# Eight dK stores sent by GpSimd in three row pieces each, in place of five dV stores in two

## The chip, the cores and the metric

The kernel runs on one core of one Trainium2 chip. The metric is the device time of one execution in microseconds; the times of several executions are given by their median. Beside them stands one execution recorded by the hardware profiler, and every duration in this document that is not a median comes from such a recorded execution. A core has five engines that are named here: TensorE (PE, with its weight loads as PEld), VectorE (DVE), ScalarE (ACT), GpSimd (POOL) and SyncE (SP, which here only issues transfers). Sixteen DMA engines move the data between HBM and the on-chip memory.

## The reference

The reference is grouped-query attention and its gradients. For 32 batches there are 32 query heads with 4 query rows each, 4 key heads with 2048 keys, and head size 128; every key head serves 8 query heads.

```
scores = einsum("bhqd,bhkd->bhqk", q, k) * scale
p = softmax(scores)
out = einsum("bhqk,bhkd->bhqd", p, v)
dq, dk, dv = vjp(out, grad_out)
```

All inputs and outputs are bfloat16. K, V, dK and dV are the large ones: 64 MiB each; q, grad_out, out and dq are small.

## The kernel before

One batch is the unit of work, and 32 batches follow each other. The four key heads of a batch are taken in two pairs, g = 0 and 1. Outside the timed program K and V are laid out so that a pair of heads is one tile of 128 partitions x 4096 elements, which a load or a store moves as 128 rows of 8192 bytes. To each K tile 128 columns are appended that hold q (pair 0) or grad_out (pair 1), so that a K row has 8448 bytes (`LONG` = 4224 elements, against `ROW` = 4096). In the same way the output tile dv1 carries the attention output in its last 128 columns, and dk1 carries dq. A batch has four loads (k0, k1, v0, v1) and four stores (dk0, dk1, dv0, dv1), some 1 MiB each. They share 20 slots of 128 x 4224 elements on the chip (`slots`, named `row` in the profile): a slot holds a loaded tile, is later written with an output tile or another input, and can be loaded again only when its store has landed.

For every batch PE transposes K and V (L260, two bf16 values moved as one 32-bit word), computes the scores (L274), after which DVE (L279) and ACT (L283) make the exponentials, and PE computes the output (L312) and dV (L334). DP = grad_out times V (L274) gives dS on DVE (L327), and from dS come dQ (L312) and dK (L334). The results leave PSUM by copies on ACT and DVE (L340); dQ is scaled and copied by DVE into the last columns of the dk1 slot (L320, `row<-psum,rs`).

GpSimd does three small things in a batch: it scales grad_out by the softmax denominator (`dop`, L290), makes the factor for dQ (`rs`, L302) and scales q (`qp`, L293). PE needs `dop` for dV and `qp` for dK.

The order of the work is written out by hand in the string `PLAN`: four characters per unit (what, part, PSUM bank or slot or copying engine, tile), read from left to right under `manual_schedule`, so that every engine runs its instructions in exactly this order. Units of neighbouring batches are interleaved: around the dQ of batch b (`y`, `z`) stand the exponentials and the dV of batch b + 1, and `F1`, the store of dk1 of batch b, follows directly behind `z`, the copy of dQ.

Loads and stores are issued by SP (L245, L350, L346), in order; an instruction on SP that waits holds back all later ones. SP's transfers run in queue q1. Five stores are an exception: dv0 of the batches 4, 6, 8, 10 and 12 (`SPREAD`) is not issued by SP but by GpSimd as an indirect DMA (`scatter`, L201 to L203), in two pieces (`PIECES`): the last 2 rows, then the first 126. They stand behind `qp` of the next batch in GpSimd's order (L295 to L299) and run in queue q0. Two tiny scatters of 3 and 13 integers (`turns`) stand ahead of the first piece and behind the last one (L205, L299). The pieces go to outputs of their own, and are put into place outside the timed program.

```
def scatter(out, in_):
    nc.gpsimd.indirect_dma_start(out=out, in_=in_, in_offset=None,
                                 out_offset=bass.IndirectOffsetOnAxis(ap=at[0:in_.shape[0], 0:1], axis=0))
```

Of the kernel before, what the change touches and what calls it, by code (L numbers as in the profile page):

```python
# [16 lines left out]
ROW = 2 * 16 * P  # L17
LONG = ROW + P
# [1 line left out]
SLOTS, E_TILES, DS_TILES = 20, 2, 2  # L20
TILES = dict(KT=8, VT=7, ET=2, DT=2)

SPREAD = (4, 6, 8, 10, 12)
PIECES = ((126, 2), (0, 126))

NAMES = dict(
    a="LK", b="LV", c="QT", d="QTe", e="KT", f="KTe", g="VT", h="VTe", i="S", j="MX", k="EX", l="RC", m="dop", n="qp",
# [141 lines left out]
def kernel(  # L169
# [13 lines left out]
    nc = tc.nc  # L183
# [14 lines left out]
    at = const_pool.tile([P, 1], mybir.dt.int32, name="at")  # L198
    nc.gpsimd.iota(at[:], pattern=[[0, 1]], base=0, channel_multiplier=1)

    def scatter(out, in_):  # L201
        nc.gpsimd.indirect_dma_start(out=out, in_=in_, in_offset=None,
                                     out_offset=bass.IndirectOffsetOnAxis(ap=at[0:in_.shape[0], 0:1], axis=0))  # L203

    scatter(turns[0], at[0:3, 0:1])  # L205
    junk = const_pool.tile([P, D], BF16, name="junk")
    slots = [const_pool.tile([P, LONG], BF16, name=f"row{i}") for i in range(SLOTS)]
    tiles = {x: [const_pool.tile([P, 8 * P], BF16, name=f"{x.lower()}_sb{i}") for i in range(n)]
# [6 lines left out]
    T = collections.defaultdict(dict)  # L215
# [17 lines left out]
    def emit(u):  # L233
# [12 lines left out]
        elif name == "QT":  # L246
            ps = t["qtp"] = bank(u)[:, 0:P]
            for j, x in enumerate(("q", "go")):
                nc.tensor.transpose(out=ps.bitcast(BF16)[:, P * j:P * j + P], in_=t[x], identity=ident[:])  # L249
        elif name == "QTe":  # L250
            t["qdt"] = sm_pool.tile([P, 2 * P], BF16, name="qdt_sb", bufs=3)
            copy16(u.where, t["qdt"][:], t["qtp"])
        elif name in ("KT", "VT", "ET", "DT"):
            x, (half, h) = name[0], divmod(i, NH) if name in ("KT", "VT") else (i, None)
            t[name, i] = tiles[name][u.tile]
            ps = t[name + "p", i] = bank(u)
            src = t[x, h] if h is not None else t["e" if x == "E" else "ds"][:]
            src = src.bitcast(FP32).rearrange("p (j d) -> p j d", d=P)
            for j in range(4):
                nc.tensor.transpose(out=ps[:, P * j:P * j + P], in_=src[:, 4 * half + j, :], identity=ident32[:])  # L260
        elif name in ("KTe", "VTe", "ETe", "DTe"):
            copy16(u.where, t[name[:2], i][:], t[name[:2] + "p", i])
        elif name in ("S", "DP"):
            if name == "S" and i == 0:
                t["S"], t["e"] = bank(u, 4), e_sb[u.tile]
            if name == "DP":
                t["DP", i] = bank(u, 2)
                if i == 0:
                    t["ds"] = ds_sb[u.tile]
            out = t["S"][:, 2 * QW * i:2 * QW * i + 2 * QW] if name == "S" else t["DP", i]  # L270
            x, side = ("KT", 0) if name == "S" else ("VT", 1)
            for w in range(2):
                for h, r in enumerate(rows):
                    nc.tensor.matmul(out[r, QW * w:QW * w + QW], lhsT=t["qdt"][:, P * side + 32 * h:P * side + 32 * h + 32],  # L274
                                     rhs=t[x, NH * i + h][:, QW * w:QW * w + QW],
                                     start=True, stop=True, tile_position=(0, 32 * h))
        elif name == "MX":
            t["m"] = sm_pool.tile([P, 1], FP32, name="m")
            nc.vector.tensor_scalar(out=t["e"][:], in0=t["S"], scalar1=-scale, scalar2=None, op0=ALU.mult,  # L279
                                    op1=ALU.min, accum_out=t["m"][:])  # L280
        elif name == "EX":
            t["l"] = sm_pool.tile([P, 1], FP32, name="l")
            nc.scalar.activation(out=t["e"][:], in_=t["S"], func=ACT.Exp, bias=t["m"][:], scale=scale,  # L283
                                 accum_out=t["l"][:])
        elif name == "RC":
            t["rinv"] = sm_pool.tile([P, 1], FP32, name="rinv")
            nc.vector.reciprocal(out=t["rinv"][:], in_=t["l"][:])  # L287
        elif name == "dop":
            t["dop"] = sm_pool.tile([P, D], BF16, name="dop_sb", bufs=2)
            nc.gpsimd.tensor_scalar(out=t["dop"][:], in0=t["go"], scalar1=t["rinv"][:], scalar2=None, op0=ALU.mult)  # L290
        elif name == "qp":
            t["qp"] = sm_pool.tile([P, D], BF16, name="qp_sb", bufs=2)
            nc.gpsimd.tensor_scalar(out=t["qp"][:], in0=t["q"], scalar1=t["rinv"][:], scalar2=scale, op0=ALU.mult,  # L293
                                    op1=ALU.mult)
            if b - 1 in SPREAD:  # L295
                for (first, count), piece in zip(PIECES, spread[SPREAD.index(b - 1)]):
                    scatter(piece, T[b - 1]["DV", "out", 0][first:first + count, 0:ROW])
                if b - 1 == SPREAD[-1]:
                    scatter(turns[1], at[0:13, 0:1])  # L299
        elif name == "rs":  # L300
            t["rs"] = sm_pool.tile([P, 1], FP32, name="rs")
            nc.gpsimd.tensor_scalar(out=t["rs"][:], in0=t["rinv"][:], scalar1=scale, scalar2=None, op0=ALU.mult)  # L302
        elif name in ("O", "DQ"):
            if i == 0:
                t[name] = bank(u)[:, 0:D]
            xt, x = ("ET", "V") if name == "O" else ("DT", "K")
            left = t[xt, i][:].rearrange("p (j q e) -> p j q e", q=P, e=2)
            for c in range(8):
                j, odd = divmod(c, 2)
                for h, r in enumerate(rows):  # L310
                    right = t[x, h].rearrange("p (j d e) -> p j d e", d=D, e=2)
                    nc.tensor.matmul(t[name][r, :], lhsT=left[:, j, r, odd], rhs=right[:, 4 * i + j, :, odd],  # L312
                                     start=(i == 0 and c == 0), stop=(i == 1 and c == 7), tile_position=(0, 32 * h))
        elif name in ("Oe", "DQe"):
            x, by, to = ("o", "rinv", "DV") if name == "Oe" else ("dq", "rs", "DK")
            t[x] = t[to, "out", 1][:, ROW:LONG]
            if u.where == "A":
                nc.scalar.activation(out=t[x], in_=t[name[:-1]], func=ACT.Copy, scale=t[by][:])
            else:
                nc.vector.tensor_scalar(out=t[x], in0=t[name[:-1]], scalar1=t[by][:], scalar2=None, op0=ALU.mult)  # L320
        elif name == "DL":
            t["dl"] = sm_pool.tile([P, 1], FP32, name="delta")
            nc.vector.tensor_tensor_reduce(out=junk[:], in0=t["o"], in1=t["go"], scale=1.0, scalar=0.0,
                                           op0=ALU.mult, op1=ALU.add, accum_out=t["dl"][:])
        elif name == "DS":
            w = slice(2 * QW * i, 2 * QW * i + 2 * QW)
            nc.vector.scalar_tensor_tensor(out=t["ds"][:, w], in0=t["DP", i], scalar=t["dl"][:], in1=t["e"][:, w],  # L327
                                           op0=ALU.subtract, op1=ALU.mult)
        elif name in ("DV", "DK"):
            i, g = divmod(i, 2)  # L330
            acc = t[name, i, g] = bank(u, 2)
            moving, still = ("e", "dop") if name == "DV" else ("ds", "qp")
            for h in (2 * g, 2 * g + 1):
                nc.tensor.matmul(acc[:, QW * (h % 2):QW * (h % 2) + QW], lhsT=t[still][rows[h], :],  # L334
                                 rhs=t[moving][rows[h], QW * i:QW * i + QW], start=True, stop=True,
                                 tile_position=(32 * h, 0))
        elif name in ("DVe", "DKe"):
            i, g = divmod(i, 2)
            copy = nc.scalar.copy if u.where == "A" else nc.vector.tensor_copy
            copy(out=heads_of(t[name[:2], "out", g])[:, :, QW * i:QW * i + QW],  # L340
                 in_=t[name[:2], i, g].rearrange("p (h c) -> p h c", h=2))
        elif name == "SK" and i in LAST:
            g, first, runs, n = LAST[i]
            part = lambda row: (row[:, 0:ROW].rearrange("p (h c) -> p h c", h=2)[:, :, first:first + n] if runs == 2
                                else row[:, first:first + n])
            nc.sync.dma_start(out=part(dk_r[g][b]), in_=part(t["DK", "out", g]))  # L346
        elif name in ("SV", "SK"):
            n = LONG if i else ROW
            if not (name == "SV" and i == 0 and b in SPREAD):
                nc.sync.dma_start(out=(dv_r if name == "SV" else dk_r)[i][b], in_=t["D" + name[1], "out", i][:, 0:n])  # L350

    with tc.manual_schedule():
# [46 lines left out]
```

## Time and profile before

| What | Value |
|---|---|
| Median of 3 runs | 669.27 us (668.84 to 670.62) |
| Profiled execution, its time | 667.87 us |
| Profiled execution, its span from first to last instruction | 665.2 us |
| Busy: PE, PEld, DVE, ACT, POOL | 605.3, 399.3, 570.6, 568.6, 51.0 us |
| Mean granted TensorE clock | 0.990 |
| Moved in the span | 273.96 MB, mean 412 GB/s |
| HBM read, written | 136.31 MB, 136.31 MB |
| GpSimd's scatters of dv0 | 10, of 937 to 1014 ns each |

The profiled execution takes 2.6 us more than its span (what lies around the first and the last instruction), and 1.40 us less than the median of the runs. In the profile a name such as `row<-in_k_dram` means that a slot is written from the input k; `out_dram<-row` is a store by SP, and `dv_dram<-row,at` a store by GpSimd. q1 holds SP's transfers, q0 GpSimd's, q8 and q14 fetch instructions and other things of the runtime. Beside the views of the page, the trace holds the landing records: each transfer posts sixteen increments of its semaphore, one from each DMA engine when its share has landed. From them one can read how far the sixteen engines are apart. The records do not give the number of the engine.

### The profile page before, as it was taken

What the parts mean: (1) busy time and instruction counts of PE and PEld (TensorE: products, weight loads), DVE (VectorE), ACT (ScalarE), POOL (GpSimd) and SP (SyncE); (2) the same over time, 40 slices, a digit from 0 to 9 for tenths busy, and PEclk for the clock granted to TensorE, in tenths of its full rate; (3) what the DMA queues carried; (4) which work ended last, traced back from release to release, by engine and by line L of the source; (5) the groups of instructions that cost most, each with busy time, mean ns of one, the idle gap of its engine ahead of it and who ended that gap; (6) DMA issues with size and microseconds to landing.
All of it is one profiled execution on the core that took longest, in us unless ns stands there. A gap on an engine that the chain in (4) does not pass through costs nothing.

```text
span 665.2 us, 20671 instructions
## 1 busy us (share of the span) xinstructions
PE 605.3 (91%) x8768; PEld 399.3 (60%) x8768; DVE 570.6 (86%) x736; ACT 568.6 (85%) x802; POOL 51.0 (8%) x115
## 2 busy tenths in 40 slices
PE   6998999999998999989999998997999988897993
PEld 5665566666665666656556665655656565565651
DVE  1988899999998899979898988887889988897893
ACT  3897899999998899979888998886988888887894
POOL 1000000101010010200000000000000000000000
PEclk9999999999999999989999999999999999999998
DMA  9999999999999999999999999999999999999967
GB/s 352 419 425 422 424 399 424 416 423 421 397 425 422 424 422 419 425 413 424 422 424 424 426 423 424 425 425 424 424 423 423 421 422 417 417 421 421 377 286 308
DMA packets 38652, 273.96 MB, mean 412 GB/s; under 512 B 4512, under 2 KB 4512, under 8 KB 6560
## 3 DMA queue, kind: packets, MB, share of 16 engines
q1 hardware_dynamic: 37536, 267.40, 96.6%
q0 software_dynamic: 1024, 5.24, 1.9%
q8 instruction: 68, 1.11, 0.6%
q14 instruction: 24, 0.20, 0.1%
HBM read 136.31 MB, written 136.31 MB: 410 GB/s over the span
## 4 chain that ended last, share of the span: by engine, by line
PE 45%; DMA 41%; ACT 5%; DVE 4%; issue 3%; SPq 0%; DVEq 0%; ACTq 0%
DMA row<-in_k_dram 38%; PE psum L260 23%; PE psum L334 10%; PE psum L312 6%; PE psum L274 6%; ACT row L340 4%; DMA row<-in_v_dram 4%; DVE vt_sb L228 3%; ACT e_sb L283 1%; DVE ds_sb L327 0%; DVE row L340 0%; DVE e_sb L279 0%; PE psum L249 0%; ACT dt_sb L226 0%; SPq L245 0%
## 5 line engine op out<-in xcount | busy, mean ns | idle before, releaser
L340 ACT CAST row<-psum 128x1024 bf16<-128x1024 f32 x292 | 289.9, 1023 | 27.2 <-PE psum L334 23.2
L260 PE MATMUL psum<-ident,row 128*128 128x128 f32 x2048 | 289.5, 283 | 25.1 <-DMA row<-in_k_dram 17.8
L260 PEld LDWEIGHTS psum<-ident,row 128*128 128x128 f32 x2048 | 224.8, 143 | 90.7 <-issue 30.5
L340 DVE CAST row<-psum 128x1024 bf16<-128x1024 f32 x220 | 264.8, 1217 | 7.2 <-PE psum L334 5.0
L226 ACT COPY kt_sb<-psum 128x512 f32<-128x512 f32 x190 | 110.2, 599 | 16.9 <-PE psum L260 16.6
L226 ACT COPY vt_sb<-psum 128x512 f32<-128x512 f32 x160 | 92.0, 602 | 35.8 <-PE psum L260 35.1
L327 DVE SCALAR_TENSOR_TENSOR ds_sb<-psum,delta,e_sb 128x1024 bf16<-128x1024 f32 x64 | 82.1, 1283 | 11.8 <-PE psum L274 7.0
L334 PE MATMUL psum<-ds_sb,qp_sb 32*128 32x512 bf16 x512 | 76.8, 383 | 3.4 <-ACT row L340 1.0
L279 DVE TENSOR_SCALAR_CACHE_REDUCE e_sb<-psum 128x2048 bf16<-128x2048 f32 x32 | 73.3, 2292 | 5.7 <-PE psum L274 5.7
L228 DVE COPY vt_sb<-psum 128x1024 bf16<-128x1024 bf16 x96 | 60.8, 685 | 13.7 <-PE psum L260 13.4
L334 PE MATMUL psum<-e_sb,dop_sb 32*128 32x512 bf16 x512 | 69.7, 384 | 2.2 <-issue 1.4
L283 ACT ACTIVATE e_sb<-psum,m 128x2048 bf16<-128x2048 f32 x32 | 64.0, 2000 | 0.2 <-DVE e_sb L279 0.2
L290 POOL TENSOR_SCALAR dop_sb<-row,rinv 128x128 bf16<-128x128 bf16 x32 | 19.4, 607 | 582.1 <-DVE rinv L287 508.4
L228 DVE COPY kt_sb<-psum 128x1024 bf16<-128x1024 bf16 x66 | 44.9, 683 | 21.4 <-PE psum L260 21.0
L260 PE MATMUL psum<-ident,ds_sb 128*128 128x128 f32 x256 | 41.9, 286 | 9.1 <-DVE vt_sb L228 6.6
L312 PE MATMUL psum<-row,dt_sb 128*32 128x128 bf16 x2048 | 43.7, 222 | 5.9 <-issue 5.3
L334 PEld LDWEIGHTS <-qp_sb 32*128 32x128 bf16 x512 | 19.4, 91 | 46.1 <-issue 42.6
L274 PE MATMUL psum<-vt_sb,qdt_sb 128*32 128x512 bf16 x512 | 40.0, 381 | 4.3 <-issue 4.2
L312 PEld LDWEIGHTS <-dt_sb 128*32 128x32 bf16 x2048 | 30.9, 95 | 21.6 <-issue 20.7
L260 PEld LDWEIGHTS psum<-ident,ds_sb 128*128 128x128 f32 x256 | 26.9, 140 | 26.6 <-DVE vt_sb L228 15.7
L226 ACT COPY dt_sb<-psum 128x512 f32<-128x512 f32 x63 | 38.4, 611 | 4.2 <-PE psum L260 4.1
L312 PEld LDWEIGHTS <-et_sb 128*32 128x32 bf16 x2048 | 30.3, 95 | 13.6 <-ACT et_sb L226 11.9
(32 smaller groups left out, 318.4 us busy)
## 6 DMA issues: line engine op xcount, KB each, us to landing
out_dram<-row SPq DMA_DIRECT2D x63, 1056.0 KB, 19.8
row<-in_k_dram SPq DMA_DIRECT2D x62, 1056.0 KB, 17.9
row<-in_v_dram SPq DMA_DIRECT2D x62, 1024.0 KB, 20.3
out_dram<-row SPq DMA_DIRECT2D x58, 1024.0 KB, 20.2
row<-in_v_dram SPq DMA_DIRECT2D x4, 512.0 KB, 9.4
out_dram<-row SPq DMA_DIRECT2D x3, 512.0 KB, 8.2
row<-in_k_dram SPq DMA_DIRECT2D x2, 544.0 KB, 5.3
row<-in_k_dram SPq DMA_DIRECT2D x2, 512.0 KB, 4.5
```

Source lines behind the costliest of these rows:

```text
L226: nc.scalar.copy(out=out.bitcast(FP32), in_=in_)
L228: nc.vector.tensor_copy(out=out, in_=in_.bitcast(BF16))
L260: nc.tensor.transpose(out=ps[:, P * j:P * j + P], in_=src[:, 4 * half + j, :], identity=ident32[:])
L274: nc.tensor.matmul(out[r, QW * w:QW * w + QW], lhsT=t["qdt"][:, P * side + 32 * h:P * side + 32 * h + 32], rhs=t[x, NH * i + h][:, QW * w: ...
L279: nc.vector.tensor_scalar(out=t["e"][:], in0=t["S"], scalar1=-scale, scalar2=None, op0=ALU.mult, op1=ALU.min, accum_out=t["m"][:])
L283: nc.scalar.activation(out=t["e"][:], in_=t["S"], func=ACT.Exp, bias=t["m"][:], scale=scale, accum_out=t["l"][:])
L290: nc.gpsimd.tensor_scalar(out=t["dop"][:], in0=t["go"], scalar1=t["rinv"][:], scalar2=None, op0=ALU.mult)
L312: nc.tensor.matmul(t[name][r, :], lhsT=left[:, j, r, odd], rhs=right[:, 4 * i + j, :, odd], start=(i == 0 and c == 0), stop=(i == 1 and c ...
L327: nc.vector.scalar_tensor_tensor(out=t["ds"][:, w], in0=t["DP", i], scalar=t["dl"][:], in1=t["e"][:, w], op0=ALU.subtract, op1=ALU.mult)
L334: nc.tensor.matmul(acc[:, QW * (h % 2):QW * (h % 2) + QW], lhsT=t[still][rows[h], :], rhs=t[moving][rows[h], QW * i:QW * i + QW], start=Tr ...
L340: copy(out=heads_of(t[name[:2], "out", g])[:, :, QW * i:QW * i + QW], in_=t[name[:2], i, g].rearrange("p (h c) -> p h c", h=2))
```

## The change

The five dv0 stores go back to SP. In their place dk1 of the batches 4, 7, 10, 13, 16, 19, 22 and 25 is stored by GpSimd, in three pieces each (two in batch 25), with the row counts that the table names. The scatters are no longer issued behind `qp` of the next batch, but at the place of `F1`, the dk1 store itself, which is behind the copy of dQ (`z`). In GpSimd's order this is between `rs` and `qp` of the next batch: for batch 4 the order becomes `dop`, `rs` (batch 5), three scatters of dk1 (batch 4), `qp` (batch 5); the first scatter waits for DVE and ACT. The scatter of 3 integers at the start goes, and the last one has 12 integers. SP issues three transfers fewer. The order of PE, DVE and ACT is the same.

```diff
-SPREAD = (4, 6, 8, 10, 12)
-PIECES = ((126, 2), (0, 126))
+SPREAD = {4: (5, 120, 3), 7: (14, 105, 9), 10: (8, 105, 15), 13: (2, 120, 6), 16: (11, 105, 12), 19: (5, 120, 3), 22: (14, 105, 9), 25: (8, 120)}
...
-    scatter(turns[0], at[0:3, 0:1])
+    if "first" in turns:
+        scatter(turns["first"], at[0:turns["first"].shape[0], 0:1])
...
-            if b - 1 in SPREAD:
-                for (first, count), piece in zip(PIECES, spread[SPREAD.index(b - 1)]):
-                    scatter(piece, T[b - 1]["DV", "out", 0][first:first + count, 0:ROW])
-                if b - 1 == SPREAD[-1]:
-                    scatter(turns[1], at[0:13, 0:1])
...
-            if not (name == "SV" and i == 0 and b in SPREAD):
+            if name == "SK" and i == 1 and b in SPREAD:
+                row = 0
+                for rows_, piece in zip(SPREAD[b], spread[b]):
+                    scatter(piece, t["DK", "out", 1][row:row + rows_, 0:n])
+                    row += rows_
+                if b == max(SPREAD) and "last" in turns:
+                    scatter(turns["last"], at[0:turns["last"].shape[0], 0:1])
+            else:
                 nc.sync.dma_start(out=(dv_r if name == "SV" else dk_r)[i][b], in_=t["D" + name[1], "out", i][:, 0:n])
...
-    spread = [[nc.dram_tensor(f"dv0_{b}_{first}_dram", (count, ROW), _mybir.dt.bfloat16, kind="ExternalOutput").ap()
-               for first, count in PIECES] for b in SPREAD]
-    turns = [nc.dram_tensor(f"turn_{n}_dram", (n, 1), _mybir.dt.int32, kind="ExternalOutput").ap() for n in (3, 13)]
+    spread = {b: [nc.dram_tensor(f"dk1_{b}_{i}_dram", (n, LONG), _mybir.dt.bfloat16, kind="ExternalOutput").ap()
+                  for i, n in enumerate(counts)] for b, counts in SPREAD.items()}
+    turns = {name: nc.dram_tensor(f"turn_{name}_dram", (n, 1), _mybir.dt.int32, kind="ExternalOutput").ap()
+             for name, n in (('last', 12),)}
```

More of the change, by code (lines that the diff above doesn't have):

```diff
@@ L392 @@
     dk0, dk1, dv0, dv1 = (_np.asarray(r.results[0][f"out_{i}_dram"]) for i in range(len(_OUTS)))
-    dv0 = dv0.copy()
-    for b in SPREAD:
-        for first, count in PIECES:
-            dv0[b, first:first + count] = _np.asarray(r.results[0][f"dv0_{b}_{first}_dram"])
+    dk1 = dk1.copy()
+    for b, counts in SPREAD.items():
+        dk1[b] = _np.concatenate([_np.asarray(r.results[0][f"dk1_{b}_{i}_dram"]) for i in range(len(counts))])
     shape = (32, 32, 4, 128)
```

## The prediction

> **What bounds the kernel now.** I read the page first. The DMA engines are busy at nine tenths or more in 38 of 40 slices, at a rate that hardly moves, and no compute engine is over 91%.
>
> ```profile
> DMA  9999999999999999999999999999999999999967
> GB/s 352 419 425 422 424 399 424 416 423 421 397 425 422 424 422 419 425 413 424 422 424 424 426 423 424 425 425 424 424 423 423 421 422 417 417 421 421 377 286 308
> ...
> q1 hardware_dynamic: 37536, 267.40, 96.6%
> q0 software_dynamic: 1024, 5.24, 1.9%
> q8 instruction: 68, 1.11, 0.6%
> ```
>
> The reader is to see a kernel at its transfer rate until the last three slices. Second, the chain that ended last, in order of time:
>
> ```profile
> 538.91 20.47 DMA row<-in_k_dram
> 559.38 0.02 issue
> 559.40 0.02 SPq L245
> 559.42 0.03 issue
> 559.45 20.46 DMA row<-in_k_dram
> 579.91 0.02 issue
> 579.93 0.02 SPq L245
> 579.95 0.03 issue
> 579.98 20.44 DMA row<-in_k_dram
> 600.41 0.14 issue
> 600.55 1.94 PE psum L260 x16
> ```
>
> A K load lands 20.5 us after its issue, SP issues another at once, and so on: SP keeps about eight transfers in flight, and each waits for the landing of an older one. PE starts 0.14 us after the landing at 600.41; from there to the end the chain is compute and stores.
>
> A landing is over when the last of sixteen engines has landed, so third I took the landing records (first, median, second last and last of the sixteen, us):
>
> ```
> first   median  second  last
> 159.00  161.47  162.70  166.88
> 166.79  172.28  174.40  174.66
> 284.14  294.71  298.33  298.42
> 458.91  467.90  470.62  471.15
> 587.82  594.76  598.72  600.41
> 661.64  661.70  661.82  663.97
> ```
>
> The engines are far apart. Following the offsets from transfer to transfer between 302 and 620 us, three kinds show. Eight take turns in losing 1.4 to 1.5 us shortly after a q8 packet. Seven lose little and run 7 us ahead of the median, with hardly any work waiting. One, which meets no q8 packet, loses 0.1 to 0.2 us again and again, 9.2 us in all: **the laggard**. It is alone at the end of each row of the table but the second and third, and never out of work, so its total work dates the landings.
>
> The table's second and third rows are behind scatters. Of the sixteen landings of a 126-row piece two come early and fourteen together (206.14 and 206.27, then 208.20 to 209.70). So 126 rows go to fourteen engines, 9 each, and the 2-row piece lies on the two left out. Five times these two carry 1 row where the others carry 9. At the first two pairs that can be followed the laggard's lag over the median falls (5.4 to 2.4 us around 161 to 172, 4.4 to 2.5 around 201 to 211), while another engine runs off to 10.6 us ahead and then idles. The laggard is one of the spared pair; the other is spared for nothing.
>
> The Trainium skill ("DMA: Bandwidth & Descriptors", Latency and other measured facts) says that DMA engines 7 and 15 are usually the slower ones. By that rule sparing engine 4 would serve no purpose. The falling lag speaks against it here.
>
> **The change, part by part.** *Rows on each engine.* I take from the 126-row piece that a piece goes to the largest number of engines up to sixteen that divides it, and that pieces follow each other around the sixteen; this fits the same pair being spared five times. Counting the old list from engine 0 (3 integers on 0 to 2) spares engines 3 and 4: 5 rows each against 40 by SP, and 45 on the other fourteen. The new list (120 rows as 15 x 8, 105 as 15 x 7) skips engine 4 in every long piece: 15 rows against 64, with 68 on engines 0 to 3 and 67 on 5 to 15. Rows follow each other at 0.3095 us (8192 bytes) and 0.3155 us (8448), from their packets:
> - engine 4: before -35 x 0.3095 = -10.83, after -49 x 0.3155 = -15.46: 4.63 us less work;
> - engines 5 to 15: before +1.55, after +0.95: 0.60 less;
> - engine 3: 12.1 us more, against a lead of 10.6 that had already been cut by idling.
>
> The Trainium skill ("DMA: Bandwidth & Descriptors", How many engines (k)) gives the same division and a cursor that goes around for transfers issued by GpSimd. The two early landings agree; that 120 and 105 rows go to fifteen engines no run here shows yet.
>
> *Loads.* The landing at 600.41 has its second-last engine at 598.72, 1.69 earlier. With the laggard 4.63 earlier (595.8) that engine becomes the last, and it is 0.60 earlier itself: 598.1, a gain of 2.3 us. PE waits only 1.1 us there, but the same shift stands at the loads before it (last over second last 1.2 to 2.1 us at 518 to 580), so PE arrives earlier too. The chain behind 600.41 names no load any more, so it moves as a whole.
>
> *The last stores.* Here SP waits for copies, and the idle fifteen engines catch up while the laggard still works off its rows: at the final landing it is 2.15 us behind (663.97 against 661.82). With 4.63 us less it has no rest left when the last stores are issued. I leave it 0.15 for its slow pace: a gain of 2.0.
>
> ```profile
> 642.77 7.79 SPq L350 DMA_DIRECT2D out_dram<-row  x4
> 652.06 6.08 SPq L346 DMA_DIRECT2D out_dram<-row  x5
> ```
>
> The reader sees that the last nine stores are issued within 15.4 us by computed results.
>
> *GpSimd.* From 12 indirect DMAs to 24: 12 more at 0.97 us, with 0.3 us between them. POOL is busy 8% of the span, so its sum costs nothing. But the first scatter of a store waits for dQ's copy, and `qp` of the next batch is behind it:
>
> ```profile
> 119.70 0.22 POOL L302 TENSOR_SCALAR rs<-rinv 128x1 f32<-128x1 f32 x1
> 120.02 0.38 POOL L293 TENSOR_SCALAR qp_sb<-row,rinv 128x128 bf16<-128x128 bf16 x1
> 120.71 0.95 POOL L202 DMA_INDIRECT dv_dram<-row,at  x1 [0.32 <-issue]
> 121.96 1.01 POOL L202 DMA_INDIRECT dv_dram<-row,at  x1 [0.30 <-issue]
> ...
> 129.07 0.12 PEld L334 LDWEIGHTS <-qp_sb 32*128 32x128 bf16 x5 [0.16 <-issue]
> ```
>
> dQ's copy ended at 124.78. Three scatters take 0.95 + 0.30 + 1.01 + 0.30 + 0.95 + 0.30 = 3.8 us, `qp` 0.38: ready at about 129.0, where PE asks at 129.07. In the other seven batches PE asks 4.3 to 4.9 us behind dQ's copy, so a stall is 0 to 0.5 us, up to eight times. Bounds: 0 and 4 us of PE. I take 0 on the end, since PE's waits for K loads, 17.8 us in 12 times, come after most of these stalls; without that cover it would be all of it. Behind `qp`, the next batch's `dop` is some 9 us away.
>
> *Queues.* Eight stores leave SP's queue, five come back: three transfers of SP fewer, and SP no longer waits for dQ's copy in eight batches (its waits for L320: 32.2 us, 11 times). As the engines are never short of work this gains nothing, bounds 0 and 1 us. Scatters took 9.3 us to land against 20 for SP's stores, that is, they pass what is queued: a load behind them is up to 2.5 us later (8 rows an engine), and as much earlier afterwards. Bytes are the same. The last such store is in batch 25, some 50 us ahead of 600; I take 0, bounds 0 and 2.5.
>
> **Sum.** 667.87 - 2.3 - 2.0 = 663.6 for the profiled execution; the median of the runs is 1.40 above it: **665.0 us**.
>
> **Rivals.**
> - *The end hardly moves*: the eight q8 engines are nearly as late (second last at 598.72), the stalls of `qp` and the passing scatters eat the 2.3, or the lag at the last stores comes back through a fetch. For it: a gap of only 1.2 us at 580. Against it: the laggard alone at 663.97. With one of the two gains: about 667.3; with neither 669.3.
> - *The wrong engine of the pair is spared* (slower). The records name no engine, so the laggard may be the one that I count as 3. It then gets 12.1 us more work, against 1.7 to 3 us by which it leads the list: the loads come some 12 us later and the last stores no sooner, 669.3 + 12 = 681. It decides if the laggard is the pair's first engine. The same holds, at up to +38 rows, if the division or the start is not as counted, and the change does not do what it says. For it: nothing in the trace tells 3 from 4. Against it: nothing but my count, so the chance is a judgement, and the weakest one here.
> - *`qp` holds PE* (slower): if a scatter took over 2 us with its wait, each `qp` would be 3 us late; PE has some 1.5 us to spare in a batch, three batches apart, so nothing is lost below about 4 us a time; at 5 us, eight times, some 8 us: 677.
>
> **Chances.** Forecast 0.60 (its own range 663.0 to 666.9); hardly moves 0.22 (666.9 to 670.5); wrong engine 0.13; `qp` 0.05. A difference of 0.3%, 2 us, is about what a measurement of this kernel can tell from no change. Faster: 0.60 and 0.04 from the lower edge of the second case, 0.64; within 0.3%: its other 0.18; slower: the last two, 0.18. The range of 8 in 10 leaves the two slow cases out: 662.5 (half a us below the forecast's own) to 670.0.
>
> **What will show it.** Right: in the landing records no engine stands alone behind the rest from 500 us on; last over second last near 600 under 1 us, and under 0.5 at the final store; q0 with 1024 rows of 8448 bytes; early landings for one engine in a 120-row piece; K loads 20.3 to 20.5 us apart. Wrong engine: one engine over 10 us behind, loads of 20.8 us. `qp`: a wait of PE at L334 for POOL of more than 1 us a batch. My forecast is wrong also if the fetches make another engine as late as the laggard was.

## The result and the profile after

The changed kernel is slower: 677.05 us (median of 6 runs, 675.64 to 678.11) against 669.91 us of the kernel before (6 runs beside it, 668.84 to 671.36), a ratio of 1.0104, with a 95% interval of 1.0085 to 1.0123. The profiled execution took 678.11 us, with a span of 676.3. Below, ratios are compared rather than times, since the kernel before has medians of 668.4 to 669.9 us in the different groups of runs.

The page of the changed kernel, the lines that answer to those shown of before:

```profile
DMA  9999999999999999999999999999999999999768
GB/s 350 420 423 425 413 387 422 423 415 424 423 410 426 423 419 407 425 424 398 421 423 421 411 423 423 405 416 421 420 398 400 425 421 395 424 420 418 297 247 317
...
q1 hardware_dynamic: 37104, 264.00, 94.5%
q0 software_dynamic: 1600, 8.65, 3.4%
q8 instruction: 68, 1.11, 0.6%
```

The engines are as busy as before, and still the rate dips: in the slices 12, 16, 19, 23, 26, 30, 31 and 34 (of 16.9 us each), where the last seven of the eight scattered stores lie, it falls to 395 to 411 GB/s. Before, it stood at 417 to 426 from the nineteenth slice to the 37th. In the windows view (a stretch and its length; busy time and instructions of each engine; granted clock; share of the DMA engines; GB/s) this is one number for each stage. The kernel before:

```profile
core 0: us, PE busy (x) PEld busy (x) DVE busy (x) ACT busy (x) POOL busy (x), PEclk, DMA share, GB/s
0.00:110.00 110.00, 97.96 (x1320) 66.86 (x1320) 84.92 (x115) 88.97 (x125) 7.87 (x23) 1.00 1.00 408
110.00:300.00 190.00, 180.94 (x2647) 119.57 (x2650) 173.29 (x225) 170.58 (x244) 22.72 (x41) 0.99 1.01 419
300.00:480.00 180.00, 166.69 (x2386) 109.84 (x2375) 158.49 (x202) 156.08 (x222) 10.46 (x27) 0.99 1.01 424
480.00:620.00 140.00, 127.56 (x1895) 83.82 (x1893) 121.88 (x157) 120.24 (x171) 7.58 (x19) 1.00 1.01 421
```

The changed kernel:

```profile
0.00:110.00 110.00, 97.29 (x1313) 66.12 (x1313) 84.38 (x114) 88.10 (x124) 6.76 (x22) 0.98 0.99 404
110.00:300.00 190.00, 180.89 (x2670) 120.02 (x2666) 174.26 (x225) 171.92 (x245) 20.16 (x38) 1.00 1.01 420
300.00:480.00 180.00, 161.85 (x2296) 107.20 (x2285) 150.07 (x192) 148.32 (x210) 18.36 (x34) 0.96 1.01 416
480.00:620.00 140.00, 128.37 (x1879) 84.89 (x1876) 120.88 (x157) 118.74 (x169) 14.01 (x27) 0.97 1.01 414
```

From 110 to 300 us the two are alike. Then 416 and 414 GB/s stand against 424 and 421 at the same DMA share of 1.01: the engines are occupied as long, but move 2% less. On 320 us that is 180 x 8/424 + 140 x 7/421 = 3.4 + 2.3 = 5.7 us. The first 110 us give 1.1 (110 x 4/408), the next stretch takes 0.5 back. So at 620 us the transfers are 6.3 us late, of the 11.1 us by which the profiled span is longer (676.3 against 665.2).

The rest lies behind the loads, and there PE's clock has a part in it. The changed kernel has the same 8768 matmuls as before, but PE is busy with them for 615.5 us, against 605.3:

```profile
PE 615.5 (91%) x8768; PEld 407.1 (60%) x8768; DVE 571.3 (84%) x736; ACT 569.6 (84%) x802; POOL 61.7 (9%) x127
```

The granted clock is the column behind POOL's. From 620 to 660 us, before and then after:

```profile
620.00:640.00 20.00, 18.75 (x273) 11.82 (x272) 18.00 (x24) 17.70 (x26) 1.20 (x3) 1.00 0.87 361
640.00:660.00 20.00, 13.38 (x271) 7.42 (x270) 14.01 (x18) 15.07 (x19) 1.20 (x3) 0.97 0.80 318
```

```profile
620.00:640.00 20.00, 18.55 (x250) 12.60 (x250) 16.89 (x22) 17.68 (x25) 1.20 (x3) 0.92 0.84 340
640.00:660.00 20.00, 19.26 (x282) 11.79 (x282) 17.15 (x22) 16.52 (x23) 1.20 (x3) 0.91 0.57 235
```

In the trace's clock records PE runs at 1.0 or at 0.5. Between 619.6 us and its last matmul the changed kernel has 13.0 us at 0.5, which is up to 6.5 us of PE's time; before has none in that part of its work. The matmul that starts at 619.6 us is 9.8 us later than the same one before, the last matmul is 14.6 us later (669.9 against 655.3), and the last stores give 3.5 back. Up to the last matmul there are 36.9 us at 0.5, against 6.8 before. Each stretch at 0.5 but the last begins 1.2 to 3.8 us after PE has fallen idle for 1.1 us or more, so in time the waits come first. But not every such wait is followed by one (before: 2.2 us idle at 606.5, and none follows), and no run changes the clock alone, so what the lower clock costs by itself is not shown.

The chain that ended last, in order of time, in the changed kernel:

```profile
542.55 1.66 PE psum L260 x14
544.21 25.55 DMA row<-in_k_dram
569.76 0.14 issue
569.89 3.65 PE psum L260 x16
```

One K load takes 25.55 us, where those of before took 20.4 to 20.5. It is the last load that the chain names (before: the one that landed at 600.41); the 106 us behind it are compute and stores. The sixteen transposes right behind it take 3.65 us, where those behind before's load took 1.94: the clock is at 0.5 from 568.4 to 575.2 us.

The landing records around it, and of the last stores, of the changed kernel (first, median, second last and last of the sixteen engines, us):

```
first   median  second  last
552.99  557.96  568.71  569.76    K load issued at 544.21
673.16  673.31  673.39  673.42    a last store
674.66  674.70  674.78  675.36    the final store
```

At the end no engine lags by itself any more: 0.03 to 0.6 us between the last two, where before had 2.15. But at the load **three** engines land 10.4 to 11.8 us behind the median (the third last at 568.36), where before, at 600.41, had one by 5.7 and the next by 4.0. The scatters of batch 25 were issued at 553.85 and 555.10 us, while this load was in flight.

### The profile page after: what moved, and what is told of

The parts are those of the page before. It is cut to its first block, busy times and chain, and to the rows that moved or that the text cites. A ratio compares the mean times of both kernels' runs of the same rounds, so it can differ in the third digit from the quotient of the medians.

```text
span 676.3 us, 20684 instructions
## 1 busy us (share of the span) xinstructions
PE 615.5 (91%) x8768; PEld 407.1 (60%) x8768; DVE 571.3 (84%) x736; ACT 569.6 (84%) x802; POOL 61.7 (9%) x127
## 4 chain that ended last, share of the span: by engine, by line
PE 56%; DMA 28%; ACT 6%; DVE 5%; issue 4%; POOL 0%; SPq 0%; DVEq 0%; ACTq 0%; POOLq 0%
PE psum L260 28%; DMA row<-in_k_dram 24%; PE psum L329 12%; PE psum L307 8%; PE psum L274 7%; ACT row L335 4%; DMA out_dram<-row 3%; DVE vt_sb L228 3%; DVE ds_sb L322 1%; ACT e_sb L283 1%; ACT vt_sb L226 0%; POOL dk_dram L201 0%; ACT kt_sb L226 0%; PE psum L249 0%; DVE row L335 0%
## 5 line engine op out<-in xcount | busy, mean ns | idle before, releaser
L260 PE MATMUL psum<-ident,row 128*128 128x128 f32 x2048 | 292.9, 286 | 25.2 <-DMA row<-in_k_dram 18.8
L260 PEld LDWEIGHTS psum<-ident,row 128*128 128x128 f32 x2048 | 227.5, 145 | 91.1 <-issue 44.5
L226 ACT COPY kt_sb<-psum 128x512 f32<-128x512 f32 x190 | 110.5, 599 | 22.0 <-PE psum L260 21.6
L228 DVE COPY vt_sb<-psum 128x1024 bf16<-128x1024 bf16 x96 | 60.7, 685 | 10.3 <-PE psum L260 10.2
L307 PEld LDWEIGHTS <-et_sb 128*32 128x32 bf16 x2048 | 31.1, 97 | 14.2 <-ACT et_sb L226 10.8
```

Of the source, the lines that this page charges most:

```text
L226: nc.scalar.copy(out=out.bitcast(FP32), in_=in_)
L228: nc.vector.tensor_copy(out=out, in_=in_.bitcast(BF16))
```

## The experiments

All are variants of the changed kernel but dv_eight, which is one of the kernel before. Each differs in the table `SPREAD` (batch: rows of each piece) and in `turns`, the scatters of integers that bring the round of engines back to where it started. The letters of the theories are those of the expectations; "theory A" means another thing from run to run. The runs were made in four groups, each on another chip and with the kernel before beside it, which is why the ratios are the measure. In the table, "late" is the landing of the 65th of the 66 K loads in SP's order, at 608 to 628 us: last and second last engine over the median, in us. "Slow rows" are rows that took more than 40 ns over the usual 319 ns (8448 bytes) or 310 ns (8192): what they took above that, summed over all engines and divided by 16.

| run | median us | ratio, 95% interval | late: last, second | GB/s 110-300, 300-480, 480-620 | slow rows, us |
|---|---|---|---|---|---|
| before | 668.4 to 669.9 | 1 | 5.8, 4.0 | 419, 424, 421 | 6.6 |
| after | 677.05 | 1.0104 (1.0085 to 1.0123) | 7.8, 6.7 | 420, 416, 414 | 12.9 |
| none | 672.82 | 1.0066 (1.0047 to 1.0086) | 8.9, 0.9 | 424, 416, 416 | 9.9 |
| early5 | 671.51 | 1.0026 (1.0002 to 1.0051) | 8.3, 6.4 | 418, 422, 418 | 8.8 |
| late5 | 674.15 | 1.0082 (1.0055 to 1.0109) | 11.8, 10.5 | 424, 414, 410 | 14.1 |
| dk_two | 672.07 | 1.0057 (1.003 to 1.0084) | 6.2, 5.0 | 421, 419, 415 | 10.7 |
| behind_qp | 675.24 | 1.011 (1.0075 to 1.0145) | 7.6, 6.7 | 419, 416, 417 | 12.1 |
| dk_one | 674.45 | 1.0095 (1.006 to 1.013) | 8.3, 1.0 | 423, 416, 414 | 10.6 |
| dk_two5 | 667.96 | 0.9984 (0.9958 to 1.001) | 5.0, 2.9 | 420, 424, 422 | 6.5 |
| dv_eight | 671.71 | 1.006 (1.0028 to 1.0092) | 6.6, 4.8 | 421, 420, 414 | 10.1 |
| dk_even | 675.83 | 1.0109 (1.0081 to 1.0137) | 9.6, 5.4 | 419, 415, 415 | 12.4 |
| dk_four | 675.85 | 1.0126 (1.0096 to 1.0157) | 9.9, 4.9 | 423, 416, 414 | 11.0 |
| dk_ints | 686.69 | 1.0266 (1.0236 to 1.0296) | 10.2, 3.3 | 412, 409, 408 | 21.6 |
| dk_two8e | 670.5 | 1.0024 (1.0003 to 1.0044) | 6.3, 6.2 | 420, 415, 418 | 11.8 |
| dk_sixteen | 677.1 | 1.0121 (1.0086 to 1.0156) | 8.9, 7.1 | 420, 413, 412 | 14.6 |
| dk_short | 674.09 | 1.0088 (1.0054 to 1.0121) | 9.5, 2.4 | 423, 417, 416 | 9.8 |
| pair_next | 667.87 | 0.9996 (0.9969 to 1.0022) | 6.5, 6.1 | 421, 423, 420 | 7.6 |
| pair_prev | 676.1 | 1.0111 (1.0077 to 1.0145) | 8.6, 1.2 | 419, 419, 416 | 10.8 |

### What is sparing an engine worth, and when?

No scatters at all:

```diff
-SPREAD = {4: (5, 120, 3), 7: (14, 105, 9), ...}
+SPREAD = {}
```

> No store by GpSimd at all: all 256 transfers by SP. Theory A (a scatter by GpSimd makes transfers slower: its rows and SP's rows take longer while both run, about 0.9 us of all sixteen engines for a dK store in three pieces, and the loads queued behind it land late): nothing of that is left here; single rows that take over 40 ns more than the usual sum to under 6 us per engine (before 6.6, after 12.9), but the slow-drifting engine keeps its whole lag, so the time is 672 to 680 with a lone engine 10 us or more behind at the last loads. Theory B (only scatters late in the kernel cost, as PE cannot win back a late K load before the end): the same. Rival C (the spreading never was of use, and every scatter costs): faster than before, 662 to 668.

It took 672.82 us, 0.66% above the kernel before and less than the changed kernel: the five scattered stores are worth some 4 us in the kernel before (rival C falls), and the changed kernel has lost all of that and more. Theory A has the time right, but not its sum of slow rows: it was to be under 6 us and is 9.9, more than before's 6.6, without any scatter. So slow rows also come with a late engine, and not from scatters alone. The windows show when the rate falls:

```profile
110.00:300.00 190.00, 180.38 (x2557) 119.92 (x2556) 171.53 (x219) 169.01 (x242) 12.02 (x30) 0.98 1.01 424
300.00:480.00 180.00, 164.85 (x2419) 108.79 (x2418) 155.47 (x199) 152.60 (x216) 9.61 (x24) 0.98 1.01 416
```

Without a single scatter the rate is 424 GB/s up to 300 us and 416 behind it. Up to then the lone late engine falls back step by step: over the median by 3.1 us at 121 us, 5.5 at 195, 8.7 at 297; from there on it stays at 8.1 to 10.0 us. At the same time the first and the last of the sixteen engines come to stand 12.5 us apart (at the K load around 340 us), and at the K loads from then on 12.2 to 13.7. At the load of the table the spread is 12.2 us in `none`, 12.6 before, 12.0 after, and 11.5 to 13.3 in every kernel. My reading is that SP's window of eight transfers holds the engines together, and that all go at the pace of the last once it is used up. That is argued, not shown: no run tried another window, the spread passes this mark for single loads (16.8 us once in the changed kernel), and before moves 421 GB/s from 480 us on at the spread at which `none` moves 416.

The five early batches of before with three pieces, and the same lists late:

```diff
+SPREAD = {4: (5, 120, 3), 6: (14, 105, 9), 8: (8, 105, 15), 10: (2, 120, 6), 12: (11, 105, 12)}     early5, no turns
+SPREAD = {13: (5, 120, 3), 16: (14, 105, 9), 19: (8, 105, 15), 22: (2, 120, 6), 25: (11, 105, 12)}  late5, no turns
```

> The changed kernel with only five of its dK stores, in the batches 4, 6, 8, 10 and 12, the piece lists being the first five. Theory A (every scatter costs about 0.9 us of transfer time wherever it stands): five eighths of the loss, 673 to 675. Theory B (early scatters are free, late ones cost): 667 to 670, as before or a little better, with PE's waits for K loads no longer than 3 us in the last 150 us. Rival C: slower than none.

> Five dK stores in the same piece lists, in the batches 13, 16, 19, 22 and 25. Theory A: the same time as the early five, 673 to 675. Theory B: all of the loss or more, 676 to 680, with PE's waits of 4 us and more for K loads behind each of them and half-clock stretches of TensorE after these waits.

The late scatters end with more loss than the early ones, 1.0082 against 1.0026, with intervals apart, as theory B has it. Its sizes are not right: the early ones are not free (671.51 us lies above its 670), and the late ones took 674.15 us, which is theory A's range and not B's 676 to 680. Whether late scatters cost more, or relieve engine 4 too late to be of use, these two runs do not tell. The profiled execution of late5 has a span of 678.7 us, above its median, so its columns are those of a bad case. The late run begins as `none` does (late: 8.6, 1.9 at 310 us) and ends with two engines 11.8 and 10.5 us late: the second one rises from 2 to 10.5 over the five scattered stores.

Which engine is late? The five early stores as 2 + 126 rows with the spared pair moved by one in each direction (the integers of `turns` set the start):

```diff
+SPREAD = {4: (2, 126), 6: (2, 126), 8: (2, 126), 10: (2, 126), 12: (2, 126)}   all three
+             for name, n in (('first', 3), ('last', 13))}                      dk_two5: spares 3 and 4
+             for name, n in (('first', 4), ('last', 12))}                      pair_next: 4 and 5
+             for name, n in (('first', 2), ('last', 14))}                      pair_prev: 2 and 3
```

> dK in two pieces (2 + 126 rows) at the changed place, but in the five early batches 4, 6, 8, 10 and 12 of the kernel before, with its two scatters of integers; against the kernel before only the stored tile and the place differ, against the eight-batch run with two pieces the number and the lateness of the batches. Theory A (pieces, and the late ones above all) expects the time of the kernel before: 668 to 670.5 us, ratio 0.998 to 1.002. Theory B (dK at this place costs in itself) expects the time of the eight early and late ones, 671.5 to 673 us, ratio 1.004 to 1.006.

> The five early dK stores as 2 + 126 rows (667.96 us, ratio 0.998), with 4 integers ahead and 12 behind in place of 3 and 13, so that the spared pair is the one counted as 4 and 5 in place of 3 and 4. Theory A (the late engine is the one counted as 4, and sparing its neighbour is worth nothing) expects the same time: 667 to 669.5 us, ratio 0.996 to 1.001, and no lone late engine at 400 us. Theory J (the engine counted as 3 is late, or sparing it counts as well) expects the loss of the single scatters, 5/8 of it, without relief: 672 to 675 us, ratio 1.005 to 1.010, one engine 8 us or more behind.

> The same with 2 integers ahead and 14 behind: the spared pair is counted as 2 and 3. Theory A expects no relief: one engine 8 us or more behind the median from 400 us on, 672 to 676 us, ratio 1.005 to 1.011. Theory J expects the time with 3 and 4: 667 to 669.5 us, ratio 0.996 to 1.001.

The answer is sharp. With 3 and 4 or 4 and 5 spared the time is that of before (0.9984, 0.9996). With 2 and 3 it is 676.1 us, 1.0111, above no scatter at all (1.0066; the intervals overlap a little). The kernel before, which spares 3 and 4, ran beside pair_next and pair_prev on one chip. So the late engine is the one counted as 4 (the first engine of GpSimd's first transfer being 0), alone, and its relief is worth 8 us when it comes early and in two pieces. (Pair_next was to have no lone late engine at 400 us; it has one 5.6 us late, with the next at 4.3.) The windows of pair_next and pair_prev:

```profile
300.00:480.00 180.00, 167.39 (x2452) 109.64 (x2449) 158.72 (x204) 156.32 (x221) 9.57 (x24) 0.99 1.01 423
480.00:620.00 140.00, 129.22 (x1909) 84.74 (x1909) 123.89 (x159) 121.75 (x175) 8.37 (x21) 1.00 1.01 420
```

```profile
300.00:480.00 180.00, 164.74 (x2430) 108.16 (x2431) 156.21 (x201) 153.66 (x218) 10.59 (x27) 0.99 1.01 419
480.00:620.00 140.00, 127.06 (x1868) 84.08 (x1866) 121.14 (x157) 119.63 (x169) 8.37 (x21) 0.99 1.01 416
```

Behind 300 us neither has a scatter. The rate differs all the same, and pair_prev has one engine 8.3 to 10.2 us late from 360 us on, pair_next 5.3 to 7.1.

### Tile, place, batches

Eight dK stores as 2 + 126 rows; eight dV stores of the kernel before in the same batches; eight early ones; and the changed kernel with its scatters behind `qp` of the next batch:

```diff
+SPREAD = {4: (2, 126), 7: (2, 126), 10: (2, 126), ..., 25: (2, 126)}      dk_two, turns 3 and 13
-SPREAD = (4, 6, 8, 10, 12)                                                 dv_eight (against before)
+SPREAD = (4, 7, 10, 13, 16, 19, 22, 25)
+SPREAD = {4: (2, 126), 6: (2, 126), 8: (2, 126), ..., 18: (2, 126)}       dk_two8e, turns 3 and 13
+            if b - 1 in SPREAD:                                            behind_qp, below tensor_scalar of qp
+                ... (the same scatters, of batch b - 1)
```

> The changed kernel's eight batches and its place behind dQ's copy, but each store as 2 + 126 rows as in the kernel before, with its tiny scatters of 3 and 13 integers. If the three pieces are the cause (fifteen engines at 8 rows, small pieces at both ends): 668 to 671, and slow rows back near 7 us per engine. If the number, the batches or the place of the stores are the cause: 675 to 679, slow rows near 12 us.

> The kernel before with its dV stores in 2 + 126 rows behind qp, but in the eight batches of the changed kernel (4, 7, ..., 25) in place of its five. Theory A (late batches cost, whatever the tile and the place) expects the 672 us of the eight dK stores in two pieces: 671 to 673 us, ratio 1.003 to 1.006. Theory B (tile and place cost, not the batches) expects the kernel before or a little better, since the drifting engine has three more reliefs: 666 to 669.5 us, ratio 0.996 to 1.001.

> Eight dK stores as 2 + 126 rows at the changed place, in the batches 4, 6, ..., 18 in place of 4, 7, ..., 25, so that all lie in the first 400 us. Theory A with its late batches (slow rows come with the late scatters; early ones relieve the late engine at little cost) expects less than the five early stores or the same: 665 to 668.5 us, ratio 0.994 to 0.999. Theory E (any store beyond five costs, wherever it stands) expects the 672 us of the eight at 4, 7, ..., 25: 671 to 673 us.

> The changed kernel with the same twenty-three pieces of dK, but issued behind qp of the next batch, as the five dV stores were before. Theory A (the loss comes from the pieces themselves: while their rows run, rows of every queue on the same engines take longer) expects no change against the changed kernel: 675 to 678 us, ratio 1.009 to 1.012, slow rows still about 12 us an engine. Theory B (the place: the scatters stand ahead of qp, which holds PE and DVE) expects most of the loss to go: 669 to 672 us, ratio 1.000 to 1.004.

The tile and the place cost nothing that can be seen: dv_eight has 1.006 where dk_two has 1.0057, and behind_qp 1.011 where the changed kernel has 1.0104 (theory B of these runs falls). Dk_two itself, 672.07 us, lies between its two ranges (668 to 671 and 675 to 679): fewer pieces give back about half of the loss. Number and lateness of the batches cost: 0.9984 with five early ones, 1.0024 with eight early ones, 1.0057 with the eight up to batch 25; the first and the last have intervals apart, neighbours overlap. Both theories for dk_two8e missed: more relief did not help further, and its 670.5 us are below the 671 to 673 of eight stores up to batch 25. Its late engines at the load of the table suggest why: the last six are 4.5 to 6.3 us late, close together. If the spared engine is one of them or ahead of them, a sixth to eighth relief has nothing left to gain; the records do not say which engine is which, so this is argued.

### What do the pieces cost?

The eight stores of the changed kernel in pieces that go to all sixteen engines alike, so that none is spared:

```diff
+SPREAD = {4: (128,), ...}             dk_one
+SPREAD = {4: (64, 64), ...}           dk_even
+SPREAD = {4: (32, 32, 32, 32), ...}   dk_four
+SPREAD = {4: (16, 96, 16), ...}       dk_sixteen
```

> The same eight dK stores at the same place, each as one scatter of 128 rows, 8 on each of the sixteen engines, so that no engine is spared. Theory A (a loss for each piece) expects a third of the loss by pieces, and the drifting engine back where it is without scatters: 673 to 676 us, ratio 1.006 to 1.010, with a lone engine last by 3 us or more at the loads late in the run. Theory B (place and passing of queued loads, whatever the number of pieces) expects as much loss as the changed kernel and no relief: 678 to 682 us, ratio 1.014 to 1.019.

> The eight dK stores of the changed kernel's batches as two scatters of 64 rows each, 4 rows on each of sixteen engines: as many pieces as 2 + 126, but no engine is spared. Theory A (each further piece makes rows beside it slow) expects the slow rows of 2 + 126 beside the scatters, about 6 engine-us a store (15 + 37 engine-us in all in that run, against 2 + 10 with one piece), and no relief: 675 to 678 us, ratio 1.009 to 1.013. Theory D (the uneven spread of the pieces over the engines makes the slow rows) expects the slow rows and the time of the single piece: about 12 engine-us beside the scatters, 673 to 675.5 us.

> The same eight stores as four scatters of 32 rows, 2 rows on each of sixteen engines. Theory A (each further piece costs) expects more slow rows than the three pieces of the changed kernel (37 + 50 engine-us beside the scatters): over 90 engine-us, and a time above the changed kernel's: 677 to 682 us, ratio 1.012 to 1.019. Theory D (uneven spread) expects the single piece's: about 12 engine-us, 673 to 675.5 us, ratio 1.006 to 1.010.

> The eight dK stores of the changed kernel's batches in three pieces of 16, 96 and 16 rows, 1 + 6 + 1 on each of sixteen engines: three scatters a store with small ones first and last, as in the changed kernel, but no engine spared. Theory A (a small price for each piece: one piece 674.45 us, two even ones 675.83, four 675.85) expects 675 to 677 us, ratio 1.010 to 1.013; the relief of the one engine in the changed kernel (677.05) would then be worth nothing. Theory H (pieces of one row on an engine cost far more, as the scatters of sixteen integers did) expects 680 to 690 us, ratio 1.018 to 1.032; the relief would then be worth the difference to the changed kernel.

One piece: 1.0095; two: 1.0109; four: 1.0126; three, with a small one first and last: 1.0121. The intervals overlap, so a price for each further piece is a tendency at most. What can be read is that **dk_sixteen, which spares no engine, takes the time of the changed kernel**: 677.1 and 677.05 us. With three pieces in eight batches the relief of engine 4 is 0.2% by the ratios, which the intervals do not tell from nothing (some 4 us could hide in them). With two pieces in the same batches it is 0.5%, some 3.5 us (dk_even to dk_two, intervals that overlap a little); with two pieces in five early ones 1.2%, 8 us (pair_prev to pair_next). Against `none`, dk_sixteen is slower by 0.55%, with intervals that just touch: three pieces in eight batches cost some 4 us where they spare no engine.

The landings of dk_sixteen and dk_one tell where it went. In dk_one a lone engine is late (8.3 us, the next 1.0). In dk_sixteen a second one is late as well, 7.1 us; in the changed kernel, where the first is relieved, the last two stand at 7.8 and 6.7. Beside the scatters (from 1 us before their first row to 1 us behind their last) the slow rows of all engines together sum to 13 engine-us with one piece, 27 with four, 52 with two even ones, 52 with 2 + 126, 74 with 16 + 96 + 16 and 88 in the changed kernel. So it is not the number of pieces: theory A was wrong in that form (its dk_four should have had over 90), and the uneven spread (D) does not explain the even pair. A large piece between small ones has most of it, and why is open.

### Small scatters

Two more scatters a store beside the single piece, of sixteen integers, and of sixteen rows of 256 bytes:

```diff
+                scatter(turns[b, 0], at[0:16, 0:1])     dk_ints: ahead of the piece, and turns[b, 1] behind it
+                scatter(turns[b, 0], ident[0:16, :])    dk_short: the same places
```

> The eight stores as one scatter of 128 rows, with a scatter of 16 integers ahead of it and one behind it: three scatters a store as in the changed kernel, but only one of them with rows of 8448 bytes. Theory A in its narrow form (what costs is rows of several pieces in flight at once) expects the single piece's 12 engine-us beside the scatters and its 673 to 675.5 us. Theory G (what costs is the number of GpSimd's scatters, by their issue and their descriptors) expects the changed kernel's 37 + 50 engine-us and 675.5 to 679 us.

> One scatter of 128 rows a store, with a scatter of 16 rows of 256 bytes (from a constant tile) ahead of it and behind it, in place of the 16 integers of the run that took 686.69 us. Theory H (the price is that of a scatter that gives an engine only one row) expects the same again: 683 to 690 us, ratio 1.022 to 1.031. Theory I (the price is that of writing 4 bytes) expects the single piece's time: 673 to 677 us, ratio 1.007 to 1.012.

The integers cost 1.7%, some 11 us (1.0266 against dk_one's 1.0095), above both ranges of dk_ints; the 256-byte rows cost nothing (1.0088). Theory G falls by dk_short, and H with it: neither the number of scatters nor one row an engine is the price. What costs is writing four bytes in place of 256 to each row. From the first integer of each of the sixteen small scatters to 2 us behind its last, slow rows of 2.4 to 36.1 engine-us start, 208 in all. That is 13 us on each of sixteen engines, about what was lost. The kernel before has two such scatters, the changed one has one: they explain none of the difference.

## Why the prediction was wrong

**The laggard's identity, and the counting of rows:** right. Pair_next and pair_prev show that it is engine 4 by that count. The prediction called the choice of 4 over 3 a judgement that nothing in the trace decides, so here it was also lucky. Queue 0 had 1024 rows of 8448 bytes, and in the first 120-row piece one landing came at 135.41 us and fifteen from 137.45 to 139.10.

**The last stores** (a gain of 2.0): right. The lone lag of 2.15 us is 0.58, and the final store lands 4.3 us after its issue, where before's took 7.0. The gain is in the time, but that store is issued 14.1 us later (671.1 against 656.96).

**The loads** (a gain of 2.3): this step failed. It read "With the laggard 4.63 earlier (595.8) that engine becomes the last, and it is 0.60 earlier itself". It took all other engines' times from the trace of before, moved by counted rows at a fixed 0.3155 us. That K load, the 64th of 66, in the two kernels (before, then after):

```
first   median  second  last
587.8   594.8   598.7   600.4
594.3   599.0   606.0   607.1
```

The median engine is 4.2 us later, not 0.6 earlier, the second last 7.3 later, and the load lands 6.7 us later in place of 2.3 earlier. The rows of the scatters themselves took 356 ns (322 in dk_one, with rows of the same size), and SP's rows beside them slowed: 50 of the 88 engine-us of slow rows beside the scatters are theirs.

**The queues** (bounds 0 and 2.5, taken as 0): the same failure seen from the other side. The text counted how many rows pass a load, and that they are given back. It did not ask whether rows take as long when pieces are mixed in, though before ran at 419 GB/s in the stretch with its five scatters and at 424 behind it: 190 x 5/424 = 2.2 us, 0.45 a store. By that row, which was in the trace, eight stores cost 3.6 us, 1.3 more than five, even if three pieces cost no more than two. (`None`, without a scatter, has 424 in that stretch.) That covers a part of the miss only. SP's waits for the copies of that line (L320 before, L315 after; O's copy as well as dQ's) did not go down either: they were 32.2 us in 11 times and are 53.0 us in 15. Dk_one, which relieves nothing, is 0.29% slower than `none`, in intervals that overlap.

**PE's clock:** the sum has no term for it, and gives no reason to leave it out. The prediction let the chain behind the last load move "as a whole". It did not: the half clock took up to 6.5 us of PE's time there. The trace of before had two examples, since the clock fell to 0.5 for 3.4 us after PE's waits of 2.6 us (at 288.3) and 2.1 us (at 462.2).

**GpSimd:** right; `qp` does not hold PE. The timeline of POOL in the changed kernel (start, duration, instruction, idle before it):

```profile
126.78 1.06 POOL L201 DMA_INDIRECT dk_dram<-row,at  x1 [5.87 <-issue]
128.15 1.01 POOL L201 DMA_INDIRECT dk_dram<-row,at  x1 [0.30 <-issue]
129.46 0.87 POOL L201 DMA_INDIRECT dk_dram<-row,at  x1 [0.30 <-issue]
130.41 0.37 POOL L293 TENSOR_SCALAR qp_sb<-row,rinv 128x128 bf16<-128x128 bf16 x1
```

And the waits of PE in the changed kernel (us in total, times, longest us):

```profile
PE psum L260 <- DMA row<-in_k_dram: 18.8, 7, 4.6
...
PE psum L329 <- POOL qp_sb L293: 1.8, 3, 0.7
```

`qp` is done at 130.8, 5.0 us behind dQ's copy. PE waited three times for `qp`, 0.7 us at most, and behind_qp, which takes that wait away, is no faster.

**The rivals.** The time, 677, is that of the `qp` rival by accident; no rival named the cause. "The end hardly moves" came nearest: it let other engines be nearly as late and "the passing scatters eat the 2.3", but priced that at 2.5 us at most. (Its gap of 1.2 us at 580 is 1.08 in the landing records.) The caveat that another engine might become as late as the laggard was the right one, with the wrong agent: not the fetches (68 packets of q8 before and after) but the slow rows beside the pieces. And the Trainium skill ("DMA: Bandwidth & Descriptors", Latency and other measured facts) says that engines 7 and 15 are usually the slower ones; here the lone late one is not in question any more, it is number 4 by the round of GpSimd's transfers. Whether the skill numbers engines in the same way no run here shows.

**What stays open:** why rows slow beside some sets of pieces and not beside others, and why that falls on one to three engines more than on the rest. Open too is the part of the clock. Up to the last matmul PE spends 6.8 us at 0.5 in before and in pair_next, 15.7 in dk_two5, 17.1 in pair_prev, 20.5 in `none`, 36.9 in the changed kernel and 44.0 in dk_ints, so it goes with the time from kernel to kernel; late loads make PE wait, but no run holds the clock fixed.

## What to carry to other kernels

An engine that is spared helps only until the next one is last, and only while the work that spares it does not make others late: read second last and third last too, and how far first and last run apart. Look at the granted clock behind a late load: the same matmuls can take longer. Price a transfer by the rate of the stretch in which its like runs (419 against 424 GB/s here), and not only by its rows times the usual duration of a row. Relieve early and in few pieces: five stores of 2 + 126 rows in the first 300 us gave 8 us over the same stores that spare the wrong pair, and some 4 over no scatter; eight of three pieces, spread to 560 us, gave nothing that could be measured.

## What the runs showed of the hardware beyond that

- Scattering sixteen 4-byte integers to HBM cost the whole core some 0.7 us a time ((1.0266 - 1.0095) x 669 / 16), though each packet lasted 9 ns; sixteen rows of 256 bytes cost nothing that could be measured.
- With one engine persistently slow and no scatter (`none`), the first engine came to stand 12.2 to 13.7 us ahead of it, and the rate of all fell from 424 to 416 GB/s at a DMA share that stayed at 1.01. Rows that took longer (9.9 us an engine over the run), and no idle time, are what the records show of it.
- Sixteen transposes of a K slot took 3.65 us in a stretch at a granted clock of 0.5 (changed kernel, behind a wait of 3.6 us for a K load), and 1.94 us at 1.0 (kernel before).
